# A finished unit's PV bank, copied by ScalarE alone or by ScalarE and VectorE in two halves of columns

## The chip, the cores and the metric

One NeuronCore of a Trainium2 chip runs the whole program. The metric is the device time of one execution in microseconds (us); three runs of the kernel before have a median of 1687.38 us (1687.36 to 1691.88).

## What is computed

One transformer block with adaptive layer norm, on 2048 rows of 512 columns, in float32:

```python
mod = (_silu(c) @ w_mod).reshape(c.shape[0], 6, 1, -1)
sa, ca, ga, sb, cb, gb = (mod[:, 0], ..., mod[:, 5])
h = _layernorm(x, axis=-1) * (1 + ca) + sa
x = x + ga * _A_ref(h, A_wqkv, A_wo)      # softmax attention, 32 heads of 16
h = _layernorm(x, axis=-1) * (1 + cb) + sb
x = x + gb * _B_ref(h, B_w1, B_b1, B_w2, B_b2)   # gelu, 1792 hidden columns
```

## The kernel before, in words

The attention is cut into 32 units (`NU`): four blocks of 512 query rows (`NB`) by eight groups of four heads (`NG`). A unit goes through its 2048 keys in 16 steps of 128 keys (`NKC`), so there are 512 steps. The order of all instructions on each engine is written out by the program itself (`half_step`, lines 1046 to 1143); no scheduler moves them.

A full step puts on TensorE:

- up to six pieces of background work, `bg_mm` (line 1024): projections, the output projection and the two layers of the feed-forward part, as half-height matmuls by line 276;
- four score matmuls `e` (`exp_mm`, line 647), each into the next of three PSUM banks (0, 1, 2). ScalarE takes the exponential of each into a tile `p` (line 654) and so frees the bank;
- four matmuls `mx` (`mx_mm`, line 390), which compute scores of a later unit for the row maximum, each into the next of three banks (3, 4, 5). VectorE reduces each bank (line 395) and so frees it;
- at the end of the step the PV matmuls of the step before, `pv` (`pv_step`, line 681; eight instructions in the trace), which add to one bank, number 6.

In many steps a VectorE copy of one column, `tick` (line 1113), tells TensorE that it may go on with the other half of the rows of its background work.

After 16 steps the PV bank holds the unit's unnormalised result and the denominators. `attn_out` (line 665) copies it to the SBUF tile `osb` (line 668), and two marks of the program's own clock later SP issues the store to DRAM (line 670). The bank has to be free before the first PV matmul of the next unit, one step later. Bank 6 is the only one of its kind and `osb` the only buffer of its kind. From DRAM the rows and denominators are read again by `o_prep` (line 716), divided, and used by the output projection.

ScalarE, VectorE and SP each run their instructions in the order in which they were written.

Of the kernel before, what the change touches and what calls it, by code (L numbers as in the profile page):

```python
# [10 lines left out]
AF = mybir.ActivationFunctionType  # L11
# [16 lines left out]
HD = D // 2  # L28
# [42 lines left out]
def block_kernel(ctx: ExitStack, tc: tile.TileContext, x, wqkv, wo, w1, b1, w2, b2, c, w_mod, out):  # L71
    nc = tc.nc
    te, ve, ac, gp, sy = nc.tensor, nc.vector, nc.scalar, nc.gpsimd, nc.sync
# [177 lines left out]
    def later(n, f):  # L251
        if n:
            hooks.setdefault(clock["t"] + n, []).append(f)
        else:
            f()
# [409 lines left out]
    def attn_out(u, pv):  # L665
        qb, g = divmod(u, NG)
        o = kqpool.tile([P, TB], F32, tag="osb", name="osb", bufs=1)
        saw(ac.activation(o, pv, AF.Copy))  # L668
        late = u < NU - 1
        later(2 * late, lambda: sy.dma_start(ou_d[qb][g], o))  # L670
        if g % 2:
            later(8 * late, lambda: ready.append((qb, g // 2)))

    def pv_step():
        s = cur["pv"]
        cur["pv"] += 1
        u, kc = divmod(s, NKC)
        if kc == 0:
            cur["ps"] = take("pv")
        for j in range(4):  # L680
            te.matmul(cur["ps"][32 * j : 32 * (j + 1)], vg[u][:, kc, j * VW : j * VW + 32], pt.pop(4 * s + j),  # L681
                      start=kc == 0, stop=kc == NKC - 1)
        if kc == NKC - 1:
            vg.pop(u)
            attn_out(u, cur["ps"])
# [333 lines left out]
    def saw(ins):  # L1019

        if act["g"] and not act["g"]["seen"]:
            act["g"]["seen"] = ins.ins
# [282 lines left out]
```

## Time and profile before

| what | value |
|---|---|
| median of three runs | 1687.38 us |
| the profiled execution | 1688.29 us, of which the program's span is 1686.5 us |
| TensorE busy | 1667.1 us (99%) |
| VectorE busy | 1403.2 us (83%) |
| ScalarE busy | 1239.3 us (73%) |
| GpSimd busy | 691.9 us (41%) |
| granted TensorE clock, mean | 0.997 |

A busy share is an average over the whole span. The chain of work that ended last tells which engine the end of the program goes back to; the timeline tells, for one engine, when each instruction started, how long it took, and, in square brackets, how long the engine was idle before it and what ended that. Successive instructions of one engine overlap a little, so the distance between two starts is shorter than a duration.

### The profile page before, as it was taken

What the parts mean: (1) busy time and instruction counts of PE and PEld (TensorE: products, weight loads), DVE (VectorE), ACT (ScalarE), POOL (GpSimd) and SP (SyncE); (2) the same over time, 40 slices, a digit from 0 to 9 for tenths busy, and PEclk for the clock granted to TensorE, in tenths of its full rate; (3) what the DMA queues carried; (4) which work ended last, traced back from release to release, by engine and by line L of the source; (5) the groups of instructions that cost most, each with busy time, mean ns of one, the idle gap of its engine ahead of it and who ended that gap; (6) DMA issues with size and microseconds to landing.
All of it is one profiled execution on the core that took longest, in us unless ns stands there. A gap on an engine that the chain in (4) does not pass through costs nothing.

```text
span 1686.5 us, 32216 instructions
## 1 busy us (share of the span) xinstructions
PE 1667.1 (99%) x12103; PEld 917.0 (54%) x12103; DVE 1403.2 (83%) x2690; ACT 1239.3 (73%) x2381; POOL 691.9 (41%) x698
## 2 busy tenths in 40 slices
PE   7999999999999999999999999999999999999999
PEld 6655555555554455555555555555555555553777
DVE  7998888889899988898999888889999889891332
ACT  3367888778777788778877888778877788779131
POOL 7433534435121456415633456306633466226110
PEclk9999999999999999999999999999999999999999
DMA  8766766757457534426453464344363453343544
GB/s 293 200 213 184 223 195 201 235 172 221 146 160 214 121 99 109 103 57 156 125 157 90 121 165 121 84 133 134 99 179 82 120 145 100 82 120 97 209 154 156
DMA packets 137127, 251.88 MB, mean 149 GB/s; under 512 B 25854, under 2 KB 45324, under 8 KB 136972
## 3 DMA queue, kind: packets, MB, share of 16 engines
q1 hardware_dynamic: 135984, 248.53, 50.9%
q8 instruction: 96, 1.57, 0.4%
q10 hardware_dynamic: 988, 1.29, 0.3%
q14 instruction: 59, 0.48, 0.1%
HBM read 188.49 MB, written 61.28 MB: 148 GB/s over the span
## 4 chain that ended last, share of the span: by engine, by line
PE 94%; DVE 3%; DMA 1%; ACT 1%; issue 0%; SPq 0%; DVEq 0%; ACTq 0%
PE bg L276 40%; PE pv L681 30%; PE e L647 16%; PE mx L390 4%; PE pr L276 2%; DVE mxp L395 2%; ACT p L654 1%; PE o L276 1%; PE mx L335 0%; DMA wm<-in_w_mod_dram 0%; DVE hTlo L484 0%; DMA wo<-wos 0%; DVE bst L237 0%; DMA kh<-qk 0%; PE mx L879 0%
## 5 line engine op out<-in xcount | busy, mean ns | idle before, releaser
L395 DVE TENSOR_REDUCE mxp<-mx 128x1 f32<-128x512 f32 x2034 | 1286.2, 683 | 145.4 <-PE mx L390 130.1
L654 ACT ACTIVATE p<-e 128x512 f32<-128x512 f32 x2048 | 1073.0, 608 | 271.7 <-PE mx L390 250.5
L390 PE MATMUL mx<-kh,qst 48*128 48x512 f32 x2034 | 836.5, 422 | 0.8 <-DVE mxp L395 0.5
L647 PE MATMUL e<-qst,kh 50*128 50x512 f32 x2048 | 778.4, 424 | 3.1 <-ACT p L654 3.1
L647 PEld LDWEIGHTS e<-qst,kh 50*128 50x128 f32 x2048 | 341.4, 185 | 430.5 <-ACT p L654 310.2
L681 PE MATMUL pv<-p,vg 128*32 128x512 f32 x4096 | 546.3, 605 | 0.3 <-ACT osb L668 0.3
L390 PEld LDWEIGHTS mx<-kh,qst 48*128 48x128 f32 x2034 | 367.8, 185 | 14.9 <-DVE mxp L395 9.7
L276 PE MATMUL bg<-w,g 64*128 64x512 f32 (+1 forms) x1056 | 263.8, 388 | 0.0
L276 PEld LDWEIGHTS bg<-w,g 64*128 64x128 f32 (+1 forms) x1056 | 196.0, 186 | 29.3
L276 PE MATMUL bg<-pchi,w 64*128 64x512 f32 (+1 forms) x656 | 177.4, 390 | 0.0
L681 PEld LDWEIGHTS pv<-p,vg 128*32 128x32 f32 x4096 | 81.0, 108 | 172.7 <-issue 159.9
L276 PE MATMUL bg<-hThi,wqkv 64*128 64x512 f32 x560 | 153.2, 392 | 0.0
L276 PEld LDWEIGHTS bg<-pchi,w 64*128 64x128 f32 (+1 forms) x656 | 120.9, 185 | 23.6 <-DVE tick L1091 4.2
L276 PEld LDWEIGHTS bg<-hThi,wqkv 64*128 64x128 f32 x560 | 103.7, 185 | 12.5
L923 POOL TENSOR_SCALAR s<-s 128x512 f32<-128x512 f32 x40 | 59.9, 1497 | 90.3 <-ACT s L921 89.6
L942 POOL TENSOR_TENSOR x<-y,x 128x512 f32<-128x512 f32 x28 | 36.1, 1288 | 144.0 <-ACT y L941 143.8
L276 PE MATMUL bg<-pclo,w 64*128 64x512 f32 (+1 forms) x328 | 88.9, 389 | 0.0
L276 PE MATMUL bg<-hTlo,wqkv 64*128 64x512 f32 x280 | 76.6, 392 | 0.0
L276 PEld LDWEIGHTS bg<-pclo,w 64*128 64x128 f32 (+1 forms) x328 | 60.0, 184 | 13.6 <-DVE tick L1091 4.2
L916 POOL TENSOR_TENSOR s<-h 128x512 f32<-128x512 f32 x40 | 41.7, 1042 | 61.9 <-ACT h L915 61.9
L276 PE MATMUL bg<-wo,pchi 64*128 64x512 f32 x192 | 59.5, 389 | 0.6 <-DMA wo<-wos 0.6
L276 PEld LDWEIGHTS bg<-hTlo,wqkv 64*128 64x128 f32 x280 | 51.6, 184 | 7.5
(164 smaller groups left out, 1324.3 us busy)
## 6 DMA issues: line engine op xcount, KB each, us to landing
kh<-qk SPq DMA_DIRECT2D x256, 192.0 KB
w<-w1s SPq DMA_DIRECT2D x56, 512.0 KB
w<-w2s SPq DMA_DIRECT2D x54, 512.0 KB
vg<-v SPq DMA_DIRECT2D x64, 332.0 KB
qk<-parts SPq DMA_DIRECT2D x32, 512.0 KB
qst<-qk SPq DMA_DIRECT2D x64, 192.0 KB
qk<-parts SPq DMA_DIRECT2D x32, 256.0 KB
ou<-osb SPq DMA_DIRECT2D x32, 256.0 KB
```

What stands on the lines that cost most here:

```text
L276: return te.matmul(ps, term[0][r], term[1][r], start=i == 0, stop=i == n - 1)
L390: te.matmul(ps, qst[u][r0 : r0 + KR, p, qc * P : (qc + 1) * P], kh(u, kr // 2)[r0 : r0 + KR, p, (kr % 2) * TB : (kr % 2 + 1) * TB], start= ...
L395: ins = ve.tensor_reduce(mxp[u][:, hc, kr : kr + 1], ps, axis=AX.X, op=ALU.max, negate=True)
L647: ins = te.matmul(ps, kh(u, kc // 8)[r0 : r0 + KX, p, (kc % 8) * P : (kc % 8 + 1) * P], qst[u][r0 : r0 + KX, p], start=True, stop=True)
L654: op = ac.activation(t, ps, AF.Exp, scale=SCALE)
L681: te.matmul(cur["ps"][32 * j : 32 * (j + 1)], vg[u][:, kc, j * VW : j * VW + 32], pt.pop(4 * s + j), start=kc == 0, stop=kc == NKC - 1)
L916: gp.tensor_tensor(s, h, h, op=ALU.mult)
L923: gp.tensor_scalar(s, s, 1.0, None, op0=ALU.add)
L942: later(4, lambda: gp.tensor_tensor(x2[t], y, x2[t], op=ALU.add))
```

## The change

The copy of the finished PV bank is split at column 256 (`HD`). ScalarE copies the first half, VectorE the second. The line numbers behind it move by one.

```diff
     def attn_out(u, pv):
         qb, g = divmod(u, NG)
         o = kqpool.tile([P, TB], F32, tag="osb", name="osb", bufs=1)
-        saw(ac.activation(o, pv, AF.Copy))
+        saw(ac.activation(o[:, :HD], pv[:, :HD], AF.Copy))
+        ve.tensor_copy(o[:, HD:], pv[:, HD:])
         late = u < NU - 1
         later(2 * late, lambda: sy.dma_start(ou_d[qb][g], o))
```

On VectorE, at the end of unit 14, the order before is as follows (`mxp` holds the maxima, `mx` is a bank; what stands in brackets is what the instruction waits for, `_49` is part of the counters' names):

```order
L1113 COPY tick<-mx 128x1 [waits PE_49]
L395 TENSOR_REDUCE mxp<-mx 128x1
L395 TENSOR_REDUCE mxp<-mx 128x1 [waits PE_49] x7
L1113 COPY tick<-mx 128x1 [waits PE_49]
L395 TENSOR_REDUCE mxp<-mx 128x1
```

And with the change, at the same place:

```order
L1114 COPY tick<-mx 128x1 [waits PE_49]
L395 TENSOR_REDUCE mxp<-mx 128x1
L669 COPY osb<-pv 128x256 [waits DMAHW3_49,Activation_49]
L395 TENSOR_REDUCE mxp<-mx 128x1 [waits PE_49] x7
L1114 COPY tick<-mx 128x1 [waits PE_49]
```

The copy stands between the last reduction of a step and the first of the next one. It waits for ScalarE (`Activation_49`), and the count that it waits for is the one that ScalarE's half of the same bank gives; the wait for a transfer (`DMAHW3_49`) is for the store of the unit before.

On TensorE, at the first PV matmul of unit 31, the order before is as follows:

```order
L276 MATMUL bg<-pchi_5350,w_22609 128x512
L647 MATMUL e<-qst,kh_192 128x512 [waits Activation_49]
L681 MATMUL pv<-p,vg 32x512 [waits DMAHW2_49,Activation_49]
L681 MATMUL pv<-p,vg 32x512 x3
L276 MATMUL bg<-pchi_5350,w_22609 128x512 [waits DVE_49]
```

And with the change:

```order
L276 MATMUL bg<-pchi_5355,w_22639 128x512
L647 MATMUL e<-qst,kh_192 128x512 [waits Activation_49]
L682 MATMUL pv<-p,vg 32x512 [waits DMAHW2_49,DVE_49]
L682 MATMUL pv<-p,vg 32x512 x3
L276 MATMUL bg<-pchi_5355,w_22639 128x512 [waits DVE_49]
```

The place in TensorE's order is the same; the bank is now given free by VectorE's copy instead of ScalarE's. The store of `osb` on SP likewise waits for VectorE instead of ScalarE.

## Rows read from the trace of the kernel before

**Rows 1.** The page, chain that ended last: shares of the span by engine.

```profile
PE 94%; DVE 3%; DMA 1%; ACT 1%; issue 0%; SPq 0%; DVEq 0%; ACTq 0%
```

**Rows 2.** Instructions on tile osb: count, shortest/median/longest ns, first and last start.

```profile
L668 ACT ACTIVATE osb<-pv x32: 597/598/678, 152.8 to 1563.9; 128x512 f32<-128x512 f32 x32
```

**Rows 3.** Timeline, TensorE, PV steps around unit ends 1 and 29: start, length us, instruction.

```profile
197.92 1.07 PE L681 MATMUL pv<-p,vg 128*32 128x512 f32 x8
200.86 1.06 PE L681 MATMUL pv<-p,vg 128*32 128x512 f32 x8
...
1483.88 1.07 PE L681 MATMUL pv<-p,vg 128*32 128x512 f32 x8
1486.72 1.06 PE L681 MATMUL pv<-p,vg 128*32 128x512 f32 x8
1489.65 1.07 PE L681 MATMUL pv<-p,vg 128*32 128x512 f32 x8
```

**Rows 4.** Timeline, ScalarE, end of unit 14 and the step behind it.

```profile
798.70 0.60 ACT L668 ACTIVATE osb<-pv 128x512 f32<-128x512 f32 x1 [0.37 <-PE pv L681]
799.19 1.57 ACT L654 ACTIVATE p<-e 128x512 f32<-128x512 f32 x3
...
802.03 2.06 ACT L654 ACTIVATE p<-e 128x512 f32<-128x512 f32 x4 [0.20 <-PE mx L390]
```

**Rows 5.** Timeline, TensorE's matmuls (PE) and weight loads (PEld), same two steps.

```profile
798.56 0.50 PE L647 MATMUL e<-qst,kh 50*128 50x512 f32 x1
...
799.83 0.18 PEld L647 LDWEIGHTS e<-qst,kh 50*128 50x128 f32 x1
799.85 0.48 PE L647 MATMUL e<-qst,kh 50*128 50x512 f32 x1
...
800.17 0.40 PE L390 MATMUL mx<-kh,qst 48*128 48x512 f32 x1
...
801.49 0.50 PE L647 MATMUL e<-qst,kh 50*128 50x512 f32 x1
...
802.81 0.18 PEld L390 LDWEIGHTS mx<-kh,qst 48*128 48x128 f32 x1
803.02 0.40 PE L390 MATMUL mx<-kh,qst 48*128 48x512 f32 x1
```

**Rows 6.** Timeline, VectorE, same two steps.

```profile
799.13 2.48 DVE L395 TENSOR_REDUCE mxp<-mx 128x1 f32<-128x512 f32 x4 [0.28 <-PE mx L390]
802.06 1.89 DVE L395 TENSOR_REDUCE mxp<-mx 128x1 f32<-128x512 f32 x3 [0.45 <-PE mx L390]
```

**Rows 7.** Groups by line and shape: count, busy us, mean ns of one, idle before.

```profile
L395 DVE TENSOR_REDUCE mxp<-mx 128x1 f32<-128x512 f32 x2034 | 1286.2, 683 | 145.4 <-PE mx L390 130.1 <-PE e L647 13.3
L340 ACT ACTIVATE vst<-mx 128x256 f32<-128x256 f32 x26 | 8.6, 384 | 0.4 <-PE mx L335 0.2
L194 DVE COPY pf<-pr 128x512 f32<-128x512 f32 x1 | 0.7, 658 | 0.0
L1113 DVE COPY tick<-mx 128x1 f32<-128x1 f32 x362 | 53.6, 148 | 0.0
L748 DVE CAST kh<-ob 128x512 fp32r<-128x512 f32 x1 | 0.4, 428 | 0.0
L844 DVE BATCH_NORM_STATS2 bsh<-x 128x6 f32<-128x256 f32 x22 | 9.1, 414 | 0.0
```

**Rows 8.** Timeline at the ends of units 8 (ScalarE, weight load) and 30 (weight load).

```profile
523.02 0.60 ACT L668 ACTIVATE osb<-pv 128x512 f32<-128x512 f32 x1
...
524.16 0.18 PEld L390 LDWEIGHTS mx<-kh,qst 48*128 48x128 f32 x1
...
1531.69 0.16 PEld L681 LDWEIGHTS pv<-p,vg 128*32 128x32 f32 x8 [0.73 <-ACT osb L668]
```

**Rows 9.** Timeline after the last unit: VectorE's last operand, TensorE's output projection.

```profile
1578.43 0.69 DVE L749 TENSOR_TENSOR kh<-ob,kh 128x512 fp32r<-128x512 f32 x1
1583.00 11.07 PE L276 MATMUL o<-wt,kh 128*128 128x512 f32 x48
```

## Prediction, before the result was known

> **What bounds the kernel now.** I read the page's chain of work first, then the instructions of the line that changes, then the timeline of each engine at the end of a unit. The reader should see in [rows 1] that 94% of the chain that ended last lies on TensorE. So the change is worth what it alters in TensorE's own pace, and shorter work on ScalarE or VectorE counts only where TensorE waits for it. The copy that the change splits takes 0.598 us, 32 times, 19.1 us in all [rows 2]; were it on the path, half of it would be a prize of 10 us. It is not: the distance from one PV step to the next shows what it costs. At the end of unit 29 the step is 1489.65 - 1486.72 = 2.93 us, and the step before it is 1486.72 - 1483.88 = 2.84; at the end of unit 1 it is 200.86 - 197.92 = 2.94 [rows 3]. Of the 32 unit ends the 27 of units 0 to 7, 10 to 24 and 26 to 29 show the same picture with the same offsets to some hundredths; unit 14 stands for them below. The split can therefore win about 0.09 us x 27, with 0.09 us at units 8, 9 and 25 as well: 2.7 us.
>
> Where the 0.09 us come from: at the end of unit 14 the copy starts at 798.70 and the next exponential at 799.19 [rows 4], 0.63 us after its score matmul at 798.56; one step later the same exponential starts at 802.03, 0.54 us after its matmul at 801.49 [rows 4, 5]. There are three score banks, so the fourth score matmul waits for that first exponential: its weights load at 799.83, 1.27 us after the step's first matmul. The fourth max matmul follows and ends at 800.17 + 0.40 = 800.57, 2.01 us into the step; one step later it ends at 803.02 + 0.40 = 803.42, 1.93 us into the step [rows 5]. So it is 0.08 us late, and the PV matmuls queue behind it.
>
> The fourth max matmul also waits for VectorE. The max banks are three as well, so it needs the bank of the step's first reduction. A reduction takes 0.683 us [rows 7], and reductions in a row start (2.48 - 0.68) / 3 = 0.60 us apart [rows 6]. In the ordinary step the first one starts at 802.06 and lasts 1.89 - 2 x 0.60 = 0.69, to 802.75, and the weight load of the fourth max matmul starts at 802.81, 0.06 us later [rows 5]: this wait already ends last there. From a load that has waited to the end of its matmul takes 0.50 us (load 799.83, matmul 799.85 + 0.48), while here it is 803.42 - 802.81 = 0.61. The first reduction thus has 0.11 us to spare and no more.
>
> **The change part by part.** *ScalarE's copy shrinks to 256 columns.* The nearest row is its copy of 256 columns out of a PSUM bank, 384 ns [rows 7]; I take that. The ends are 0.30 (half of 0.598 [rows 2]) and 0.598. Either of the first two frees ScalarE before the exponential could start, so the 0.08 us go. *VectorE gets a copy of 256 columns*, 32 times. In the built order it stands behind a reduction and ahead of the next step's three or four, and carries a wait for ScalarE's half. So the two halves run one after the other, and the reductions queue behind both.
>
> Its price has no row of its own. VectorE's copy of 512 columns out of PSUM took 658 ns and its copy of one column 148 [rows 7], 1.0 ns a column, which makes 403 ns. Successive reductions start 0.08 us before the one ahead ends (0.60 against 0.68, above), so the copy holds the queue for 0.32 us. Bounds: 0.21 us by the copy of 512 columns from SBUF to SBUF, 428 ns [rows 7] (148 + 140 - 80), and 0.38 by the other operation on 256 columns, 414 ns [rows 7], with a smaller overlap of 0.03. I take 0.32, since its rows read PSUM and copy.
>
> *Unit 14 with these numbers.* ScalarE's half ends at 798.70 + 0.384 = 799.08. With 0.05 us of hand-over (as from the reduction to the load above) VectorE starts at 799.13 and is free at 799.45. The first reduction stands at 799.13 now, after 0.28 us of idle time [rows 6], so it moves by 0.32 us: the idle time is there, but the wait for ScalarE uses it up. It ends at 799.45 + 0.68 = 800.13, the load of the fourth max matmul starts at 800.18, and the matmul ends at 800.68. That is 0.11 us later than the 800.57 of now. VectorE's reductions of that step end by about 801.9 (four of 0.60 from 799.45, and a tick), before the next step's first one at about 802.17, so nothing carries over. 27 x 0.11 = **3.0 us**.
>
> *Units 9 and 25.* A batch_norm row of 256 columns follows the copy on VectorE and now fills the idle time without delay; it would start only after the copy, and the first reduction after it: 0.11 + 0.33 (414 ns less the overlap [rows 7]) = 0.44 each, **0.9 us**.
>
> *Unit 8* has no background matmuls. The load of its fourth max matmul stands at 524.16, 1.14 us after the copy's start at 523.02 [rows 8]; by the arithmetic above it would stand 1.48 after it, **+0.3 us**.
>
> *Unit 30.* No reductions are left there. The next unit's first PV matmul waits for the single PV bank: its load at 1531.69 was released by the copy [rows 8]. Two halves in series take 0.384 + 0.05 + 0.40 = 0.83 us in place of 0.60: **+0.2 us**.
>
> *The last unit.* The denominators and rows take the way through DRAM; the last operand of the output projection is written by 1578.43 + 0.69 = 1579.12, and that projection begins at 1583.00 [rows 9]. The 0.2 us that the copy ends later are covered by those 3.9 us, and would cost 0.2 without them.
>
> *The store of the bank* on SP now waits for VectorE's half, 0.2 us later. What is queued behind it are loads for the next unit, whose steps are 2.84 us each [rows 3] and many; cost nothing, and at most these 0.2 us where a load is used at once. ScalarE's half gains a wait for VectorE's copy of the unit before, 45 us old: nothing.
>
> **Sum:** 3.0 + 0.9 + 0.3 + 0.2 = +4.4 us. The profiled execution took 1688.29 us (its span is 1686.5), which gives 1692.7; the median of the runs shown is 1687.38, 0.9 lower, so I predict **1691.8 us**, 0.26% above. A measurement of this kernel tells about 0.3%, 5.1 us, from no change: I expect a small loss that counts as the same.
>
> A rule stands against the change whatever the prices. No row of the trace of before has ScalarE and VectorE at one PSUM bank together. The Trainium skill, PSUM — Partial Sum Buffer, section "PSUM bank collisions raise a hardware error", says that two engines may not read the same bank and partitions at once, disjoint columns included, and that software must order them; by it a split by columns cannot be made parallel, and no run here shows it. Were the halves parallel, the sum would be the second rival's.
>
> **The rivals.** *VectorE's share decides: slower by over 0.3%.* The place is the same first reduction. Each 0.01 us of the copy's slot costs 0.30 us over the 30 unit ends, so the loss passes 5.1 us from a slot of about 0.345 us. At the upper bound, 0.38, it is 27 x 0.17 + 2 x 0.50 + 0.4 + 0.3 = 6.3 us: 1693.7. For it: the row of 414 ns is VectorE's nearest by size, and reductions read PSUM at 0.60 us for 512 columns. Against: the copy of 512 columns itself was shorter than a reduction.
>
> *The halves run side by side: a gain.* Then VectorE's copy would fill the 0.28 us of idle time before the reduction, and the 0.08 to 0.09 us at 30 units would go: -2.5 us, 1684.9. Against it stands the wait in the built order, on every one of the 32 copies.
>
> *The loss is smaller.* At the lower bound, 0.21 us, the first reduction moves by 0.21 us only, the fourth max matmul ends where it does now, and units 8, 9, 25 and 30 alone cost 0.2 + 0.7 + 0.1 = 1.0 us: 1688.4. Against it: VectorE's rows on PSUM are at 1.0 ns a column and over.
>
> **How the numbers follow.** Forecast 0.60; slot of 0.345 us or more 0.25; smaller loss 0.11; side by side 0.04. A gain of over 0.3% would need 5.1 us where at most 2.7 lie, so faster gets 0.02 for what I don't see. Slower gets 0.25 and a part of the forecast's upper tail, 0.30; the same gets the rest, 0.68. The range goes from 1687.8, under the smaller loss, to 1694.2, over the upper bound; the side-by-side case and 1 in 10 at the top are left out.
>
> **What would show it.** In the profile after: VectorE's copy near 0.40 us and starting about 0.05 us behind ScalarE's half of 0.38; the first reduction behind it about 0.75 us after ScalarE's start, where it is 0.43 now; PV steps at unit ends of about 3.04 us in place of 2.93, others still 2.84; 3.4 at units 9 and 25. The prediction is wrong if VectorE's copy starts with ScalarE's, if those steps are 2.85 or shorter, or if steps away from the unit ends change.

## The result, and the profile after

The changed kernel took 1693.0 us (median of 12 runs, 1690.93 to 1694.59), the kernel before beside it 1688.55 (12 runs, 1687.27 to 1691.88). The ratio is 1.0022, with a 95% interval from 1.0014 to 1.0030: a small loss. The interval leaves out no change at all, and the loss is less than the 0.3% that the prediction took for what a measurement can tell. The profiled executions have spans of 1690.6 us after and 1686.5 before, 4.1 us apart.

The chain that ended last, in the page of the kernel after:

```profile
PE 92%; DVE 3%; DMA 2%; ACT 1%; issue 1%; POOL 0%; SPq 0%; POOLq 0%; DVEq 0%; ACTq 0%
```

It still lies on TensorE [rows 1]. The busy times of the page after:

```profile
PE 1671.2 (99%) x12103; PEld 921.5 (55%) x12103; DVE 1413.6 (84%) x2722; ACT 1235.8 (73%) x2381; POOL 691.9 (41%) x698
```

VectorE has 1413.6 us instead of 1403.2. ScalarE's 19.1 us of copies [rows 2] have become 12.4 us, 6.7 less, and VectorE has 13.6 us of copies that it did not have. Tile `osb` after, in the columns of [rows 2], and the two groups by shape:

```profile
L668 ACT ACTIVATE osb<-pv x32: 384/385/465, 152.6 to 1567.9; 128x256 f32<-128x256 f32 x32
L669 DVE COPY osb<-pv x32: 424/425/426, 153.1 to 1568.3; 128x256 f32<-128x256 f32 x32
```

```profile
L669 DVE COPY osb<-pv 128x256 f32<-128x256 f32 x32 | 13.6, 425 | 24.6 <-ACT osb L668 24.5
L668 ACT ACTIVATE osb<-pv 128x256 f32<-128x256 f32 x32 | 12.4, 388 | 12.4 <-PE pv L682 12.2
```

VectorE stood idle for 24.6 us ahead of its copies, 24.5 of them until ScalarE's half had ended. 14.9 of these lie at the last two units, where VectorE has no other work; at most of the others it is about 0.28 us. All 32 copies start 0.03 us behind the end of ScalarE's half: the halves do run one after the other.

The end of unit 14 in the timeline of the kernel after: ScalarE, VectorE, then TensorE's PV steps and the weight load of the fourth max matmul.

```profile
800.52 0.38 ACT L668 ACTIVATE osb<-pv 128x256 f32<-128x256 f32 x1 [0.39 <-PE pv L682]
800.91 1.58 ACT L654 ACTIVATE p<-e 128x512 f32<-128x512 f32 x3
...
799.97 0.68 DVE L395 TENSOR_REDUCE mxp<-mx 128x1 f32<-128x512 f32 x1
800.93 0.42 DVE L669 COPY osb<-pv 128x256 f32<-128x256 f32 x1 [0.28 <-ACT osb L668]
801.27 2.48 DVE L395 TENSOR_REDUCE mxp<-mx 128x1 f32<-128x512 f32 x4
...
799.38 1.06 PE L682 MATMUL pv<-p,vg 128*32 128x512 f32 x8
802.43 1.06 PE L682 MATMUL pv<-p,vg 128*32 128x512 f32 x8
...
802.01 0.18 PEld L390 LDWEIGHTS mx<-kh,qst 48*128 48x128 f32 x1 [0.19 <-DVE mxp L395]
```

The copy starts 0.03 us after ScalarE's half ends (800.52 + 0.38 = 800.90). The first reduction follows 801.27 - 800.93 = 0.34 us later, 0.75 after ScalarE's start, where it was 0.43 [rows 4, 6]. It ends at 801.27 + 0.68 = 801.95; the load of the fourth max matmul stands at 802.01, after an idle time that the trace now puts down to a reduction (`DVE mxp L395`). The step is 802.43 - 799.38 = 3.05 us; before it was 2.94.

From the starts of such PV rows, at all unit ends:

| place | before | after | difference, all of them |
|---|---|---|---|
| 27 regular unit ends, mean (shortest to longest) | 2.938 (2.92 to 2.97) | 3.053 (3.05 to 3.06) | +3.1 us |
| units 9 and 25 | 2.93, 2.93 | 3.38, 3.385 | +0.9 |
| unit 8 and the step behind it | 2.704 + 2.846 | 2.618 + 2.882 | -0.05 |
| unit 30 and the step behind it | 2.488 + 2.403 | 2.741 + 2.121 | -0.03 |
| the 478 other steps together | | | +0.26 |
| first PV step to last | | | +4.19 |

The stretch ahead of the first PV step is 0.16 us shorter and the one behind the last 0.02 longer, so the 4.19 us become the 4.05 by which the span grew.

### The profile page after: what moved, and what is told of

It is laid out like the page before. It is cut to its first block, busy times and chain, and to the rows that moved or that the text cites. A ratio compares the mean times of both kernels' runs of the same rounds, so it can differ in the third digit from the quotient of the medians.

```text
span 1690.6 us, 32276 instructions
## 1 busy us (share of the span) xinstructions
PE 1671.2 (99%) x12103; PEld 921.5 (55%) x12103; DVE 1413.6 (84%) x2722; ACT 1235.8 (73%) x2381; POOL 691.9 (41%) x698
## 3 DMA queue, kind: packets, MB, share of 16 engines
q8 instruction: 96, 1.57, 0.4%
## 4 chain that ended last, share of the span: by engine, by line
PE 92%; DVE 3%; DMA 2%; ACT 1%; issue 1%; POOL 0%; SPq 0%; POOLq 0%; DVEq 0%; ACTq 0%
PE bg L276 40%; PE pv L682 29%; PE e L647 16%; PE mx L390 4%; DVE mxp L395 2%; ACT p L654 1%; PE pr L276 1%; PE o L276 1%; DMA kh<-qk 1%; PE mx L335 0%; DMA wm<-in_w_mod_dram 0%; DVE bst L237 0%; DMA wo<-wos 0%; DMA qst<-qk 0%; PE mx L880 0%
## 5 line engine op out<-in xcount | busy, mean ns | idle before, releaser
L395 DVE TENSOR_REDUCE mxp<-mx 128x1 f32<-128x512 f32 x2034 | 1285.8, 682 | 130.2 <-PE mx L390 114.2
```

The source lines that it names most:

```text
L395: ins = ve.tensor_reduce(mxp[u][:, hc, kr : kr + 1], ps, axis=AX.X, op=ALU.max, negate=True)
```

## The experiments

My theory: the second half waits for the first, and VectorE's queue holds the step's first reduction behind that wait; TensorE stops at the fourth max matmul for it. Rivals: VectorE's copy costs by its work, wherever it stands and whatever it waits for; half a copy on ScalarE is itself what hurts or helps; or the store of `osb`, which leaves later, is what costs. Each ratio below is against the kernel before on the same chip (1689.3 us, 27 runs, for the first four; 1689.43, 21 runs, for the last three). The diffs are against the changed kernel, except for the last one.

**One half alone.** Two kernels do one half and nothing else, on a tile `osb` that is set to 1.0 once at the start (the lines for that are left out of the two diffs).

ScalarE's half alone:

```diff
         saw(ac.activation(o[:, :HD], pv[:, :HD], AF.Copy))
-        ve.tensor_copy(o[:, HD:], pv[:, HD:])
```

> ScalarE copies columns 0 to 255, and nothing copies the others: that half of the stored result stays at a constant 1, so the attention output of half the query rows is left out. Theory (the loss comes from the two halves in series, which make the step's first reduction late): ScalarE's half frees ScalarE in time, no reduction moves, PV steps at unit ends fall from 2.93 to 2.84-2.85 us, total about 2.6 us under the kernel before, ratio 0.9984. Rival (VectorE's added work costs by itself, 0.34 us x 32 on an engine 84% busy): also about -2.6 us here, this run alone does not separate them. Rival (the copy's cost on ScalarE was never the 0.09 us): ratio 1.000, steps stay at 2.93.

VectorE's half alone:

```diff
-        saw(ac.activation(o[:, :HD], pv[:, :HD], AF.Copy))
-        ve.tensor_copy(o[:, HD:], pv[:, HD:])
+        saw(ve.tensor_copy(o[:, HD:], pv[:, HD:]))
```

> VectorE copies columns 256 to 511, and nothing copies the others: that half of the stored result stays at a constant 1, so the attention output of the other half of the query rows is left out. Theory (series): VectorE's half starts with the end of the PV matmuls, fits into the 0.28-0.30 us of idle time before the first reduction, which stays at about 0.43 us after the copy's start; unit-end steps 2.84-2.86 us, total about 2.6 to 2.9 us under the kernel before, ratio 0.9983. Rival (VectorE's added work costs by itself): VectorE carries the same 32 copies as in the changed kernel, so unit-end steps near 2.97-3.05 and a ratio of 1.001 to 1.003.

The first: ratio 0.9993 (0.9985 to 1.0002), steps of the 27 units 2.837. The second: 0.9981 (0.9972 to 0.9990), steps 2.843. Unit 14 in the timeline of the second, ScalarE, VectorE and TensorE's PV steps:

```profile
799.98 1.57 ACT L654 ACTIVATE p<-e 128x512 f32<-128x512 f32 x3 [0.80 <-PE mx L390]
...
799.62 0.41 DVE L672 COPY osb<-pv 128x256 f32<-128x256 f32 x1
800.01 2.48 DVE L395 TENSOR_REDUCE mxp<-mx 128x1 f32<-128x512 f32 x4
...
798.45 1.07 PE L685 MATMUL pv<-p,vg 128*32 128x512 f32 x8
801.29 1.07 PE L685 MATMUL pv<-p,vg 128*32 128x512 f32 x8
```

Without a wait for ScalarE the copy fills the idle time that VectorE has there anyway, and the step is that of an ordinary place, 2.84; ScalarE is idle for 0.80 us until TensorE's matmul, so TensorE sets the pace here. So the 0.41 us of work cost nothing at the regular unit ends, and neither half slows the kernel; the loss needs both, in series. Only at units 9 and 25 does VectorE's half alone cost something (3.00), since the batch_norm row is still behind it.

**The order turned round.** VectorE's half first, ScalarE's behind it.

```diff
-        saw(ac.activation(o[:, :HD], pv[:, :HD], AF.Copy))
         ve.tensor_copy(o[:, HD:], pv[:, HD:])
+        saw(ac.activation(o[:, :HD], pv[:, :HD], AF.Copy))
```

> Both halves, but VectorE's is written first and ScalarE's waits for it. Theory (series): now the reduction is on time and the wait sits on ScalarE: its half starts about 0.43 us after the PV matmuls, the step's first exponential about 0.72 us after them instead of 0.50, the fourth score matmul and behind it the fourth max matmul are late by 0.22 us more than before; unit-end steps about 3.15 us, total about +6 us, ratio 1.0037. Rival (VectorE's added work costs by itself): as the changed kernel, unit-end steps 3.05, ratio 1.0022. Rival (the later store): the same as the changed kernel.

Ratio 1.0042 (1.0028 to 1.0056), most steps 3.23, mean 3.246. Unit 14, ScalarE, VectorE, TensorE:

```profile
803.79 0.39 ACT L669 ACTIVATE osb<-pv 128x256 f32<-128x256 f32 x1 [0.89 <-DVE osb L668]
804.07 1.57 ACT L654 ACTIVATE p<-e 128x512 f32<-128x512 f32 x3
...
803.34 0.41 DVE L668 COPY osb<-pv 128x256 f32<-128x256 f32 x1
803.71 2.48 DVE L395 TENSOR_REDUCE mxp<-mx 128x1 f32<-128x512 f32 x4
...
802.14 1.06 PE L682 MATMUL pv<-p,vg 128*32 128x512 f32 x8
805.38 1.06 PE L682 MATMUL pv<-p,vg 128*32 128x512 f32 x8
```

The wait has changed engines: ScalarE now starts when VectorE has ended (803.34 + 0.41), the reduction is on time, and the first exponential comes 1.93 us into the step instead of 1.53. The loss was sized too low, because VectorE is still in the reduction before when the bank is finished: its copy starts 803.34 - 803.20 = 0.14 us after the PV step's end.

**VectorE does it all.**

```diff
-        saw(ac.activation(o[:, :HD], pv[:, :HD], AF.Copy))
-        ve.tensor_copy(o[:, HD:], pv[:, HD:])
+        saw(ve.tensor_copy(o, pv))
```

> VectorE copies all 512 columns, ScalarE nothing. Theory (series): the copy starts with the end of the PV matmuls and holds VectorE for 0.58 us, the first reduction starts about 0.59 us after it instead of 0.43 (0.76 in the changed kernel), the fourth max matmul ends 0.03 us later than in an ordinary step; unit-end steps about 2.87 us, units 9 and 25 about 3.2, total about -1.3 us, ratio 0.9992. Rival (VectorE's added work costs by itself): twice the work of the changed kernel's half, so slower than it, steps over 3.1, ratio 1.004 or more.

Ratio 1.0000 (0.9991 to 1.0009), most steps 2.95. Unit 14, VectorE and TensorE:

```profile
800.21 0.68 DVE L668 COPY osb<-pv 128x512 f32<-128x512 f32 x1
800.81 2.47 DVE L395 TENSOR_REDUCE mxp<-mx 128x1 f32<-128x512 f32 x4
...
799.02 1.07 PE L681 MATMUL pv<-p,vg 128*32 128x512 f32 x8
801.97 1.07 PE L681 MATMUL pv<-p,vg 128*32 128x512 f32 x8
```

Again a little too hopeful, by the same late start: the reduction begins 1.79 us into the step. But twice the work on VectorE makes the regular steps 2.96 on average, 0.12 us over the 2.84 of e1 and e2, where half of it behind ScalarE makes them 3.05, 0.21 over. The rival by which VectorE's work sets the price falls: the work is free only as far as VectorE is idle there, but even the whole copy costs less than half of it behind the wait.

**The wait with next to no work.** ScalarE copies everything, as before; VectorE copies the last column again.

```diff
-        saw(ac.activation(o[:, :HD], pv[:, :HD], AF.Copy))
-        ve.tensor_copy(o[:, HD:], pv[:, HD:])
+        saw(ac.activation(o, pv, AF.Copy))
+        ve.tensor_copy(o[:, TB - 1 :], pv[:, TB - 1 :])
```

> ScalarE copies all 512 columns as before, and VectorE then copies the last column once more, 0.07 us of its queue, waiting for ScalarE. Theory (series): the wait does most of the harm, since the first reduction cannot start before ScalarE's copy has ended: about 0.70 us after ScalarE's start in place of 0.43 (0.76 in the changed kernel); unit-end steps about 3.00 us (before 2.94, changed 3.05), units 9 and 25 about 3.3, total about +2.5 us, ratio 1.0015. Rival (VectorE's added work costs): a fifth of the changed kernel's work, so unit-end steps 2.94 to 2.96 and under +0.9 us, ratio 1.0005 or less.

Ratio 1.0011 (1.0002 to 1.0020), steps 3.002. VectorE in unit 14:

```profile
800.03 0.16 DVE L669 COPY osb<-pv 128x1 f32<-128x1 f32 x1 [0.50 <-ACT osb L668]
800.10 2.48 DVE L395 TENSOR_REDUCE mxp<-mx 128x1 f32<-128x512 f32 x4
```

One column, 0.07 us of VectorE's queue, makes the step 0.064 us longer than before, against 0.115 for the split. The wait itself is longer here, for ScalarE's whole copy (0.50 us of idle time against 0.28), so the two numbers do not divide the split's loss into wait and work. They do show that a copy of next to no length is dear behind the wait: 0.16 us over the 2.84.

**The same two halves, the second one later.** VectorE's half goes behind the next step's first reduction, by the program's own clock, where the store also stands.

```diff
         saw(ac.activation(o[:, :HD], pv[:, :HD], AF.Copy))
-        ve.tensor_copy(o[:, HD:], pv[:, HD:])
         late = u < NU - 1
+        later(2 * late, lambda: ve.tensor_copy(o[:, HD:], pv[:, HD:]))
```

> The change, but VectorE's half is written behind the first reduction of the next step (two marks of the program's clock later), with the same wait for ScalarE's half. Same work, same wait, another place. Theory (series in front of the first reduction): the wait is over when VectorE comes to it and the first reduction is on time, the later reductions have room; unit-end steps 2.84-2.86 us, units 9 and 25 too, total about -2.6 us, ratio 0.9984. Rival (VectorE's added work, wherever it stands): as the changed kernel, steps 3.05, ratio 1.0022.

Ratio 0.9986 (0.9978 to 0.9995): 1686.87 us, faster than both kernels; steps 2.840, at units 9 and 25 too. Unit 14, ScalarE, VectorE, TensorE:

```profile
799.16 0.39 ACT L668 ACTIVATE osb<-pv 128x256 f32<-128x256 f32 x1 [0.40 <-PE pv L682]
799.55 1.58 ACT L654 ACTIVATE p<-e 128x512 f32<-128x512 f32 x3
...
799.59 0.69 DVE L395 TENSOR_REDUCE mxp<-mx 128x1 f32<-128x512 f32 x1 [0.32 <-PE mx L390]
800.20 0.41 DVE L670 COPY osb<-pv 128x256 f32<-128x256 f32 x1
...
798.03 1.07 PE L682 MATMUL pv<-p,vg 128*32 128x512 f32 x8
800.87 1.06 PE L682 MATMUL pv<-p,vg 128*32 128x512 f32 x8
```

The work is that of the changed kernel, instruction by instruction. The reduction goes first, 1.56 us into the step; when the copy's turn comes, at 800.20, ScalarE's half has been done since 799.55, so nothing waits. The store rival falls here too: in unit 14 the store of `osb` starts 2.61 us into the step, later than in the changed kernel (2.00) and in the kernel before (1.76), and this kernel is the fastest of the three.

**ScalarE's whole copy later.** The same idea without VectorE: the copy of the kernel before, put behind the next step's first exponential. The diff is against the kernel before.

```diff
-            attn_out(u, cur["ps"])
+            pv = cur["ps"]
+            later(int(u < NU - 1), lambda: attn_out(u, pv))
```

> The kernel before, with ScalarE's whole copy written behind the first exponential of the next step instead of ahead of it; VectorE has no part. Theory (what the old copy cost was the lateness of that one exponential): the exponential starts 0.40 us after the PV matmuls' end plus hand-over instead of 0.50, the later ones have room; unit-end steps 2.84-2.86 us at the 27 units and at 8, 9 and 25; at unit 30 the next PV matmul waits up to 0.5 us longer; total about -2.3 us, ratio 0.9986. Rival (the copy costs ScalarE's time wherever it stands): steps stay at 2.93, ratio 1.000.

This missed: 1.0033 (1.0021 to 1.0046). Steps at the unit ends did fall to 2.840, but the step behind each grew by about 0.3 us. The 27 regular unit ends with 9 and 25 give -2.8 us, the 478 other steps +8.3, and units 8 and 30 with the steps behind them +0.3: together +5.8, where the ratio gives +5.6. Unit 14, ScalarE and TensorE's weight loads for that PV step:

```profile
802.54 0.60 ACT L654 ACTIVATE p<-e 128x512 f32<-128x512 f32 x1 [0.77 <-PE mx L390]
803.04 0.59 ACT L668 ACTIVATE osb<-pv 128x512 f32<-128x512 f32 x1
803.51 1.09 ACT L654 ACTIVATE p<-e 128x512 f32<-128x512 f32 x2
...
803.84 0.14 PEld L681 LDWEIGHTS pv<-p,vg 128*32 128x32 f32 x4 [0.34 <-ACT osb L668]
804.17 0.14 PEld L681 LDWEIGHTS pv<-p,vg 128*32 128x32 f32 x4 [0.18 <-ACT p L654]
```

The next unit's first PV matmuls now follow the copy itself, and their second four the exponential that the copy had pushed back. The copy only moved from ahead of one thing that TensorE waits for to ahead of another.

**One picture of all.** At the end of unit 14, how long after the PV step's start ScalarE's first exponential and VectorE's first reduction begin, and how long the step is (e1, e2 and so on are the runs in the order above; in e7 the cost lies in the step behind this one):

| kernel | first exponential | first reduction | step |
|---|---|---|---|
| before | 1.63 | 1.57 | 2.94 |
| e1, e2, e6, e7 | 1.52 to 1.53 | 1.56 to 1.57 | 2.83 to 2.84 |
| e4 | 1.53 | 1.79 | 2.95 |
| e5 | 1.63 | 1.84 | 3.01 |
| after | 1.53 | 1.89 | 3.05 |
| e3 | 1.93 | 1.57 | 3.24 |

Where the reduction is late, the step is its start plus 1.16 or 1.17 us (e4, e5, after); where the exponential is late, it is that start plus 1.31 (before, e3); where both are early it is 2.83 to 2.84, and there ScalarE and VectorE wait for TensorE (0.80 us of idle time ahead of the exponential in e2, 0.32 ahead of the reduction in e6). In each row the step is the longest of the three. The changed kernel trades the exponential, which kept the step 0.10 us over that, for the reduction, which keeps it 0.21 us over.

Steps and ratios agree, but for e1. From the unit ends (27 regular ones, 9, 25, and 30 with the step behind it) the sums are -3.1 us for e1, -2.9 for e2, +8.7 for e3, +0.8 for e4, +2.5 for e5 and -2.8 for e6; the ratios give -1.2, -3.2, +7.1, 0.0, +1.9 and -2.4, with some 1.5 us of uncertainty either way (2.4 for e3). For e1 the steps give more than the interval allows. Its profiled execution spends 0.9 us more ahead of the first PV step (107.7 against 106.8), and its runs had lower mean granted clocks than those of the kernel before (0.993 to 0.997 against 0.993 to 0.999); at 0.997 its three runs have a median of 1686.3 against 1688.7 for five, 2.4 less.

## Why the prediction was right, and where it was not

Forecast: 1691.8 us, a loss within 0.3%, from a sum of +4.4 us. Measured: 1693.0 us, 1.2 more, because the base was that much too low: three runs of the kernel before had a median of 1687.38, the twelve beside the changed kernel 1688.55. The spans of the profiled executions are 4.1 us apart, the medians 4.45. The mechanism that the prediction named, the wait of VectorE's half ahead of the step's first reduction, is the one that the runs show.

- **ScalarE's half.** 384 ns forecast, 385 measured. The 0.08 us that it had cost went: the first exponential starts at 1.53 us into the step instead of 1.63, and e1, with only this half, has steps of 2.84.
- **The two halves in series.** Forecast from the built order, with a hand-over of 0.05 us; 0.03 measured, at all 32. In the kernel after and in e3 the second reader of the bank starts 0.03 to 0.04 us behind the end of the first, in either order; this is the wait of the built order. The prediction's sentence that no row of before has both engines at one bank says more than rows can show, since they name the tile `mx` and not which of its banks. No row contradicts the rule that the prediction drew from the Trainium skill, PSUM — Partial Sum Buffer, section "PSUM bank collisions raise a hardware error", and what two readers at once would do no run here shows. The rival of halves side by side is thus ruled out for this program only: each run that reads the bank from two engines has the wait.
- **The slot of VectorE's copy.** 403 ns long and 0.32 us of queue forecast; 425 ns and 0.34 measured. The forecast took the line through one column (148 ns) and a single copy of 512 (658 ns); e4's copies of 512 took 677 to 692. The slot is 0.02 us longer and the hand-over 0.02 shorter than forecast, so the first reduction starts 0.75 us after ScalarE's half, as forecast: the two misses cancel, and that is luck. So it came to 0.115 us a unit end instead of 0.11, 3.1 us for 3.0. The first rival began at 0.345 us, so the middle of the bounds was right by a narrow margin.
- **Units 9 and 25.** 0.44 each forecast, 0.445 and 0.454 measured. VectorE there, after:

```profile
570.67 0.42 DVE L669 COPY osb<-pv 128x256 f32<-128x256 f32 x1 [0.28 <-ACT osb L668]
571.01 0.42 DVE L845 BATCH_NORM_STATS2 bsh<-x 128x6 f32<-128x256 f32 x1
571.34 2.47 DVE L395 TENSOR_REDUCE mxp<-mx 128x1 f32<-128x512 f32 x4
```

- **Unit 8: the step failed.** The prediction has "by the arithmetic above it would stand 1.48 after it" and +0.3 us for it. The load of the fourth max matmul stands 1.05 us after the copy's start (it was 1.14 [rows 8]), and the step became 0.09 us shorter. ScalarE's copy starts at 523.61; VectorE and the loads after:

```profile
524.37 1.28 DVE L395 TENSOR_REDUCE mxp<-mx 128x1 f32<-128x512 f32 x2
...
524.66 0.18 PEld L647 LDWEIGHTS e<-qst,kh 50*128 50x128 f32 x1 [0.65 <-ACT p L654]
524.66 0.18 PEld L390 LDWEIGHTS mx<-kh,qst 48*128 48x128 f32 x1
```

The load comes while the first reduction still runs (to about 525.05), so it does not need that bank. In a step without background work one of the four max matmuls goes into the bank of the background work (`"bg" if free`, line 1128 of the kernel before; the reduction at 525.57 reads `bg`). The fourth then takes the third bank of the ring, which the last reduction of the step before gave free by 523.91, and only the exponential sets the place. The arithmetic of the regular step was carried to a place with another ring.
- **Unit 30: the size was right, the step behind it was not looked at.** +0.25 us for the +0.2 forecast, and then -0.28 in the next step. The rows after, ScalarE, VectorE, TensorE:

```profile
1535.01 0.47 ACT L668 ACTIVATE osb<-pv 128x256 f32<-128x256 f32 x1
1535.27 1.18 ACT L654 ACTIVATE p<-e 128x512 f32<-128x512 f32 x2
...
1535.50 0.42 DVE L669 COPY osb<-pv 128x256 f32<-128x256 f32 x1 [1.96 <-ACT osb L668]
...
1533.24 1.07 PE L682 MATMUL pv<-p,vg 128*32 128x512 f32 x8
1535.98 1.06 PE L682 MATMUL pv<-p,vg 128*32 128x512 f32 x8 [0.55 <-DVE osb L669]
1538.10 1.06 PE L682 MATMUL pv<-p,vg 128*32 128x512 f32 x8
```

The PV matmuls do wait for the later half, 0.55 us instead of 0.30. But the step behind had room. Before, it took 2.40 us where the steps around the pair take 2.12 to 2.13; after, it takes 2.12, so it has absorbed the lateness. The half copy on ScalarE is not needed for that: e5, with the whole copy on ScalarE, has 2.680 + 2.216, in sum the 4.89 to 4.90 of before. Nor is it enough: e1, whose exponentials are just as early as those of the changed kernel but whose bank is free sooner, has 2.276 + 2.408. e2 and e4, without a copy on ScalarE, have the shortest pairs, 2.121 + 2.285 and 2.126 + 2.281.
- **The last unit and the store.** Nothing was forecast for either. The stretch behind the last PV step is 0.02 us longer, and the 478 other steps together 0.26. In e1, which has no copy on VectorE, these steps are 0.20 longer too, so the 0.26 is not put down to the change.

The terms of units 8 and 30 come to +0.5 us in the forecast and to -0.08 in the trace, and the 0.1 of the regular unit ends and the 0.26 of the other steps go the other way. That the sum of 4.4 lies so near the 4.2 from the first PV step to the last is in part luck; the answer would have been the same without these errors.

## What to carry to other kernels

The two engines that copied one bank here made a chain, not a pair: price the second half by what stands behind it in its engine's queue while it waits, and not by its own work alone. Over the 2.84 us of an undisturbed step, one column behind the wait cost 0.16 us, half the columns behind it 0.21, all of them without a wait 0.12, and half of them without a wait nothing. Then place it: the same two halves gave 1.0022 with the second ahead of the reduction that TensorE waits for, and 0.9986 behind it. And before moving a copy behind one consumer, list everything else that waits for the instructions that it then stands ahead of; ScalarE's copy, moved without that, lost at every unit's next step what it had won.

## What the runs showed of the hardware that was not expected

A VectorE instruction that starts after idle time takes some 10 ns longer in these traces than one that follows another directly. Copies out of PSUM that follow directly took 146 to 150 ns for one column (most of `tick`), 414 to 415 for 256 (e6) and 677 to 681 for 512 (most of e4's); after idle time they took 157 to 160, 424 to 426 and 690 to 692. The reductions do the same, 681 ns against 692. So the copies lie on two straight lines, both of 1.04 to 1.05 ns a column. The 403 ns of the prediction came from the single row of 658 ns in [rows 7], and the copies of the changed kernel started after idle time. In the queue 256 columns held VectorE for 0.34 us, 512 for 0.60.

A stall of the same length can cost TensorE its clock or not. In unit 10 TensorE waits in all nine profiles, at a DMA share of 0.93 to 1.08 in the stretch of the stall. In e5 the granted clock stays at 1.00 behind it, the upper of the two levels (2.4 GHz); in e4 it reads 0.62 and 0.53 in the next two stretches, and in e2 0.50, the lower level (1.2 GHz). Below are stretches of 2 us, with the length, the busy time of TensorE, its weight loads, VectorE, ScalarE and GpSimd (and their instructions), the granted clock, the DMA share and GB/s; e5, then e4:

```profile
579.00:581.00 2.00, 1.19 (x8) 0.51 (x7) 2.00 (x4) 1.56 (x4) 0.01 (x1) 1.00 1.07 247
581.00:583.00 2.00, 2.00 (x15) 0.68 (x14) 2.00 (x5) 0.80 (x2) 0.00 (x0) 1.00 1.04 244
```

```profile
579.00:581.00 2.00, 1.20 (x4) 0.48 (x3) 2.00 (x4) 1.57 (x4) 0.06 (x1) 1.00 1.08 235
581.00:583.00 2.00, 2.00 (x11) 0.65 (x12) 1.94 (x4) 0.36 (x1) 0.00 (x0) 0.62 1.01 266
583.00:585.00 2.00, 2.00 (x10) 1.06 (x8) 1.62 (x3) 1.57 (x3) 0.00 (x0) 0.53 1.14 215
```

TensorE was busy for 1.19 and 1.20 of the 2 us ahead. In the profiles of e2, e4 and e6, where the clock fell there, one or two steps are 1.0 to 1.3 us longer than in the kernel before; in those of before, after, e1, e3, e5 and e7 it did not fall. Why it falls in one execution and not in another stays open. The clock goes with a part of the scatter between runs: of the 27 runs of the kernel before, the four with a mean clock of 0.994 have a median of 1690.3 us, the five with 0.997 one of 1688.7 and the two with 0.999 one of 1687.2, but the two with 0.998 lie at 1689.6. A difference of 2 us is therefore read from the steps, and from many runs, but not from two spans.
